# A new order table for a fused attention and two-layer kernel on one core

## The chip, the cores and the metric

The kernel runs on one core of a Trainium2 chip. The metric is the device time of one execution in microseconds. The engines spoken of are PE (TensorE, the 128 x 128 matmul array), DVE (VectorE), ACT (ScalarE), POOL (GpSimd) and SP (SyncE, which here only issues DMA transfers).

## The reference

For each of 4 batches of 12,480 tokens with 128 channels, 32 learned vectors attend to the tokens, and the tokens then attend to the 32 results. What comes out goes through two linear layers (128 to 2048 to 128) with a leaky rectifier that has one slope per hidden unit between them.

```
h   = mab(I, x)          # softmax(scale * I x^T) x, 32 rows
o   = mab(x, h)          # softmax(scale * x h^T) h, 12480 rows
u   = o @ w_in           # 128 -> 2048
g   = max(u, 0) + alpha * min(u, 0)
out = g @ w_out          # 2048 -> 128
```

## The kernel before

**Tiling.** Tokens are taken in groups of 512; a batch has 24 such groups and one of 192, so there are 100 groups in all. The 32 rows of h are multiplied into w_in once per batch (`hW`, 32 x 2048), so the first layer has a contraction of only 32: its operands are `hW` and the exponentials `rep`. Every matmul of both layers uses one *row tile* of the array, 32 of its 128 rows, and the four row tiles work side by side. The letters w, x, y and z name row tiles 0 to 3.

**Fill.** One `fill` computes 128 hidden units for 512 tokens: one matmul of `rep` and `hW` on one row tile into one of eight accumulation banks. ACT (line 772) or DVE (line 774) then applies the rectifier and writes the result to a buffer `gt` in bfloat16, which frees the bank. The table says which of the two does it. A full group has 16 fills.

**Second layer.** Each `gt` buffer has 128 rows, and `second` multiplies it with `W1` in four matmuls, one per row tile, all of which add into one bank that belongs to the group. A row tile's *part of a group* is 16 such matmuls. The parts of w, x, y and z follow each other on the group's bank: x begins when w has ended, and so on. Since two row tiles may not write one bank at once, `second` calls `hand_over` ahead of the first matmul of x, y and z: PE's queue waits there until the last matmul of the tile before has finished. Within a tile the parts of successive groups follow without a break. When z has ended its part, DVE transposes the bank (`ot`, line 845), POOL scales it (`ob`) and issues the stores. The last three groups take whole 128-row matmuls instead.

**The other work.** At 36 pauses, numbered by batch and 2048-token block, PE, ACT and DVE do the attention work of this and the next batch: scores and their exponentials (`bs`, `as`), sums into h (`aa`), denominators (`den`). Ahead of a batch's first group stands a chain: `hd` inverts the sums of the softmax (`rh`, `fr` on DVE), `ht` makes h (`hT`), `hw` multiplies h into w_in. SP then writes the exponentials to memory (`e2d`), reads them back to all four row tiles (`rep`) and does the same for the denominators (`rt`, `rdT`).

**Order.** All instructions are pinned to the order in which the code records them, on every engine. That order is the string `PLAN`: a to h with a digit is a fill (row tile by pairs of letters, the first of a pair evacuated by ACT, the second by DVE; the digit is the bank), w to z is the next second-layer matmul of that row tile, l opens a group's bank, v is a whole matmul, s is the next pause, and the digits after it are its banks. `PAUSES` lists what is done at each pause in order; `EVENTS` lists loads and transfers by group and fill.

```
        first = i < LATE and n == 0 and not r
        if r and n == 0:
            hand_over(left[i])
        ins = mm(
            home[i][:, :t], W1[rows, c, :], gt[rows, :],
            start=first, stop=False, skip_group_check=True,
        )
```

Of the kernel before, what the change touches and what calls it, by code (L numbers as in the profile page):

```python
# [38 lines left out]
20 8 bs06 aa15 den05 hd1  # L39
21 4 ht1  # L40
21 12 hw1 bs10 as20 den06 hl1
# [171 lines left out]
zyd3l6zyxwzya0xzyb1xzywxzya2zxyzxwys3012xh4ywxg3ywxywh0xywg2xe1wxwzf4xwzxwe3zxwzf2xwzc0wzd1wyzwy
c4zyza3yzxb2yzxl0yzxwyzc1b4yzxwyzxa3yzxwyg2xwyxwh1yxg4wyxwyxg3wyd7wxwe2zxwf1zxwzxwe4zxwf3zc7wzc2
ywzyd1zyxzya4xzb3yxza7yxzyxb2zyxzl1yxg4wyxwh3yxwg7yxzwyxzwyc2ywxg4yxwf3xwze7xwzxwf2s5437wyzd2wyz
c5wyzwyzd4we3zwyzb7yza2yzxya5zxyb4zxyl3zxywxzf7a2xzywxzywxg5ywxg4ywxyh2wxg7wxwxzf5wxze6wxze4wxzw
zd2wzywzc7ywzd6ywzyc5za4yzb2xyzxyl7zxywzxyb6g5xywzxywzxya4xywg2xywh6xywxywg5xwf4xwze0xwzf2xwze6x
wzwzd5ywzc4ywzc0ywzyl6zd2wzyxwzyxzya4xzyb5xzya0xzywxg2ywxzywxywh4xywg5xywxyg0wxs2154wxe0zwxf2zwx
e1zxwze4d5zwzywd0zywc2zyl1yzxwyzxa5zyxb4zyxwyzc2b0yzxwyzxa5yxwzyxwg4yxwg2yxwh0yxwyxwg5xwf4xzwe3x
zwxzwf2c0zwzd5ywyzwyzc4l3yzwxzya2xzyb0xzywxe5zwd4yzwxzya2xzywxzya0xywxh5ywxg4ywxywxg2ywxh0wxe7zw  # L220
xf4zwxzwe5c2zwyzwd0yzl7ywzxya4xzf5wzxywyzc2b0yzxwyzxa4yzxb5yzxwzyc2wzyxs0452ywxg0f6wxg4ywxg5ywxh
2ywxs0d6we4zxwzxwze5xwzf2c0wzd4zyl6yxzwxyza5xyzb2xyzwc0yzwxyzb4xyza5xyzwxyza2xyzwxywg0xyh4wxyg5x
wys21045wxywxh2e1wxf4zwc5zwyzwyc0zwyd1zwyc2zyzb5xyza4xyzl0xyzwxyza1xf2zwxzywxf4g5wxyzwxyza1xzywx
yg2wxyg5wxyh4wxwxf1zwxe3zwzwc2yzwyd5wzyc4wzyzl3d1yzwxyza2xyzwxf5zwxe4zwxyzb1xyza2xywzxyzwc5ywxyg
4wxyg1b2xywxywxe5b7xzwe4xzwd2zwxe1zwd5zwyc7zwyzc4yb2zxyl1zxywzxya5h7yxwzyxwg4d2ywzywxza5yxzyb7xz
xywg4ywxzywxg2yxwe5wxf7wzxf4xzws2657wxzf2wzc4wzyd6wzyc7l5zywwzxywwwzxe2b4zxywwzxywa7h6xywwxzywwx
zwe2wb4xyzwxwzya7xzyl6xywxg2ywxyh4wxywg7xywxwf0c2zwyxzxwxyxh4wc7yzxwyxzxwxe2d0zwyxzxwyxzwc7f4zxw
yxzxwyc2zb0yxzxxyza7xyzb4xyzxya2zxyzl0xywg7xywxyh4ywyxe2zwxyzwyxyyh3we7xzwyxyzywyxe4h2wxyzwyxyyz
wyc7f3zwyzwyc4zwyd2zwyzwc7yzyb3zxya4zxyzxa2yzxl7yzxzwyzzxa3zf4zxzwzyzxzwzyg2xywh1xwyzxg3wyxzzwxz
ze4wzxf2wzxwe1zxwzf3c5wzywzyc4wzyd2wzyc1zwyb3zyza5xyzxyb4zxya2zxyl1xzywxze3xwyh5xwyg4xwyxwyg2xwy  # L230
h3s6452xzwf3xzwe6xzwe4xzwf2xzwc5zwzwyd3wzywd6zywc4zya2zyl5zyxwh3yxwzyxwg4yxb6zyxwzyxa2yzxwyxwyg3
xwyxh4ya6xwe2xwxzf0wxzwxe3zwxzf6wzc4wzywd2zywc0zyzya3zxb6yzxyl4zxywzc2b0yzxywzxya3zxywg6xywxyh2w
xywg0xyg3wxywh7xwe6xzwxzwf2xzwe0xzwd3zwyzc7wyzwyza6d2yzl0xyzwxyg3wd7yzwxyzwxe6zb2xyzwxyza3xyzwxy
a7xywh6xyg2wxywxyg3wxf1wxwzxe7wzxf2zwc6zwyzwd3yzc1yzxa7yzxb2yzxl6yzxwyzc3b1yzxwyzxwyg7xb2yzxwyzx
we3zwxyg1wxywxywxh7ys23517xwzf2xwze3xwzf7c5wzwzyc1wzyd2wzya3zyzyxb7zyxa5zyxb1zyxl2zyxwze3xwzyd7w
yxg5wyxzwyxg1wyxg3wyxh7wyxwxg5wxzf1wxze4wxzwzd3wzyc7wzyd5wzyc1l4zyxwzyxa3zf7xwzyxwze1xzb5yxzwyxz
a3yxzwyxg7wyxwh1yxa5yxwg3yxwyxh0wyxwe7xwzf5wc1zywzywd3zywc0zya7zyxb5zyxl1zyxwzyc3b0zyxwzyxwg7f5x
wzyxwzyxa3zf0xwzyxwg7yxwzyxwg5yxwf3xwe0zxwzxwze7wd6zywzywc5yzd0l3zwxe7zwxzyb6xzywc5yzwxyzxb0yzxa
7zyxwyh6xa5yzxwyzxwyg0xwyxwg7yxwyh5xws60275h6we0xwzxwzd2e5zyc7wzywzyd0l6zyxwzyxa5zyd2wzyxwg7yxwz
f0xwzyxa5zyxwh2yxwze7xwzyxwh0yxa5yzxwyxza2yxg7wxwzxf0wze5wzywd2zywc4zya7zyxzb0yxzl5yxzwyxg2b4yxz  # L240
wyxzwyc7h0wyxzwyxza2yxh4wyxzwyc7zwyxzwe0xwf2zxwzxe4wzxwzxe7wzd0wzywzc1yl4zd2ywzxya7zxywh0xywzc1y
wzyxb2zyxa7zyxwzyxa0zyxwg1yxwyxwh2yxwg7yxwxf0we3xzwf1xzwze2xwzwzc7wyzd0yl3zwyxzya2xh1ywxzxya7zxy
b0zxywzc2wyzd1wyzxa7yzwxyzwxyg0wxyh2xwyg1wxye7wxwxzf0s6127f0zxwe6zxwzd1we7zwyzc2yzxyb0zxyzxya6zy
xb7zyxa1zyxl2zyd0wzyxwg6yxwh7yxwzyc1wzyxwg0yxwh6xywxwe7xzwxe1zwxzwf0c5zwyzwd7yzwc6yzwd1yza0yzxl5
yzxwyzxa7f6zxwyzxwyg0xb1yzxwyzxa7yzxwyg6xwyh0xwyxg1wyxwe7xwzxf4wzxe6wzwzyd1wzyc0wzyd7wzya4zya6xz
yxzb1yxzl0yxzwyd7zwe4xzwyxzwe6xzwyxg1wyxwh4yxwyg7xwyxh6wyxa3xe1wzxwzf4xwze7wzywzd3ywzc6yl1zyxwh4
yxwg7yxwzyxb3zyc6wzyxwzyxa4h7yxwzyxwzyd3a6zyxwzyxwg4yxwzxe7wzxwzxb6s34273e6wzd4f7wzxe2wzxs3yc6wz
yl4zd2ywzxya7zxzb3yxg6wyxywzxwyh2xyg7wxzwyxzb3yc6ywzxyzwxza2yxyg7wxwyxf6xg3wxwze2xwzf5zwzwyc7zwy
# [902 lines left out]
```

## Time and profile before

| what | value |
|---|---|
| time, 3 runs | 540.28, 542.75 and 543.44 us; median 542.75 us |
| the profiled execution | 540.08 us, with a span of 538.2 us from its first to its last instruction |
| PE busy | 523.0 us |
| DVE busy | 503.5 us |
| ACT busy | 495.8 us |
| POOL busy | 395.7 us |
| granted clock | 0.998 |

Busy time is the union of an engine's instructions, so that matmuls which run side by side count once, and an ACT or DVE instruction that starts before the one ahead has ended counts only for what it adds. A PE that is busy all the time can still have free row tiles.

### The profile page before, as it was taken

What the parts mean: (1) busy time and instruction counts of PE and PEld (TensorE: products, weight loads), DVE (VectorE), ACT (ScalarE), POOL (GpSimd) and SP (SyncE); (2) the same over time, 40 slices, a digit from 0 to 9 for tenths busy, and PEclk for the clock granted to TensorE, in tenths of its full rate; (3) what the DMA queues carried; (4) which work ended last, traced back from release to release, by engine and by line L of the source; (5) the groups of instructions that cost most, each with busy time, mean ns of one, the idle gap of its engine ahead of it and who ended that gap; (6) DMA issues with size and microseconds to landing.
All of it is one profiled execution on the core that took longest, in us unless ns stands there. A gap on an engine that the chain in (4) does not pass through costs nothing.

```text
span 538.2 us, 21998 instructions
## 1 busy us (share of the span) xinstructions
PE 523.0 (97%) x9275; PEld 333.5 (62%) x9276; DVE 503.5 (94%) x865; ACT 495.8 (92%) x994; POOL 395.7 (74%) x574
## 2 busy tenths in 40 slices
PE   4999999999999999999999999999999999999995
PEld 4655566666567666666667666666666566666652
DVE  3699999999999999999999999999999999999994
ACT  2499999999999999999999999999999999999950
POOL 5553777787678988688687987776777877776764
PEclk9999999999999999999999999999999999999999
DMA  8998999986898988787799797855344344334324
GB/s 196 213 185 138 163 198 149 185 141 117 131 170 144 146 152 151 163 129 143 116 161 161 123 163 154 157 114 113 67 93 113 66 95 113 70 90 108 66 43 85
DMA packets 114738, 71.14 MB, mean 132 GB/s; under 512 B 86784, under 2 KB 102784, under 8 KB 114640
## 3 DMA queue, kind: packets, MB, share of 16 engines
q0 software_dynamic: 19456, 38.62, 39.0%
q1 hardware_dynamic: 91984, 30.22, 32.9%
q8 instruction: 72, 1.18, 1.0%
q10 hardware_dynamic: 3200, 0.90, 0.7%
q14 instruction: 26, 0.21, 0.1%
HBM read 41.00 MB, written 28.95 MB: 130 GB/s over the span
## 4 chain that ended last, share of the span: by engine, by line
PE 90%; DMA 4%; DVE 2%; ACT 2%; POOL 1%; issue 1%; SPq 0%; POOLq 0%; DVEq 0%
PE bank L385 90%; DMA xn<-in_x_dram 2%; ACT gt L772 1%; DVE gt L774 1%; DMA rep<-e2d 1%; POOL xn L414 1%; DVE ot L845 0%; DVE xT L463 0%; SPq L673 0%; PE bank L460 0%; DVE fr L610 0%; DVE ob L853 0%; POOL out_dram L878 0%; ACT e L658 0%; ACT rep L683 0%
## 5 line engine op out<-in xcount | busy, mean ns | idle before, releaser
L385 PE MATMUL bank<-gt,W 32*128 32x512 bf16 x6255 | 478.7, 371 | 0.3 <-ACT e L658 0.2
L772 ACT ACTIVATE gt<-bank 128x512 bf16<-128x512 f32 (+1 forms) x906 | 464.1, 617 | 5.6 <-PE bank L385 3.7
L774 DVE TENSOR_SCALAR gt<-bank 128x512 bf16<-128x512 f32 (+1 forms) x662 | 417.5, 678 | 8.7 <-PE bank L385 5.0
L385 PE MATMUL bank<-rep,hW 32*128 32x512 bf16 (+1 forms) x1600 | 418.9, 368 | 0.5 <-DMA rep<-e2d 0.3
L385 PEld LDWEIGHTS <-W 32*128 32x128 bf16 x6256 | 264.6, 92 | 145.1 <-issue 43.5
L878 POOL DMA_DIRECT2D out_dram<-ob x386 | 248.1, 672 | 37.0 <-POOL ob L853 29.4
L853 POOL TENSOR_TENSOR ob<-ot,rdT 128x512 f32<-128x512 f32 (+2 forms) x99 | 106.6, 1077 | 90.8 <-DVE ot L845 88.1
L385 PEld LDWEIGHTS <-hW 32*128 32x128 bf16 x1600 | 136.8, 92 | 19.9 <-issue 5.5
L845 DVE STREAM_TRANSPOSE ot<-bank 128x512 f32<-128x512 f32 (+1 forms) x100 | 69.9, 699 | 5.0 <-PE bank L385 4.0
L385 PE MATMUL bank<-rep,hA 32*128 32x512 bf16 (+1 forms) x100 | 36.1, 367 | 0.0
L429 POOL DMA_DIRECT2D xn<-in_x_dram x32 | 20.7, 663 | 0.1
L483 ACT ACTIVATE e1t<-bank 128x256 bf16<-128x256 f32 (+2 forms) x14 | 5.0, 358 | 10.9 <-PE bank L385 10.9
L463 DVE COPY xT<-bank 128x1024 bf16<-128x1024 bf16 (+1 forms) x13 | 8.4, 651 | 5.1 <-PE bank L460 4.6
L385 PE MATMUL bank<-xT 32*128 32x512 bf16 x81 | 12.5, 376 | 0.0
L555 ACT ACTIVATE e<-bank 128x512 bf16<-128x512 f32 x18 | 11.1, 616 | 0.2 <-PE bank L385 0.2
L658 ACT ACTIVATE e<-bank 128x512 bf16<-128x512 f32 x18 | 11.1, 617 | 0.1
L385 PEld LDWEIGHTS <-xT 128*128 128x128 bf16 (+1 forms) x177 | 7.9, 95 | 4.3 <-issue 1.5
L385 PEld LDWEIGHTS <-hT 128*32 128x32 bf16 (+1 forms) x122 | 3.7, 93 | 10.9 <-issue 10.8
L385 PE MATMUL bank<-xT,hT 128*32 128x512 bf16 (+1 forms) x98 | 10.3, 388 | 0.0
L385 PEld LDWEIGHTS <-hA 32*128 32x128 bf16 x100 | 9.2, 92 | 1.7 <-issue 0.8
L460 PE MATMUL bank<-ident,xn 128*128 128x128 bf16 x96 | 8.6, 242 | 1.4 <-DVE xn L990 0.9
L414 POOL DMA_DIRECT2D xn<-in_x_dram x11 | 6.2, 581 | 3.3 <-DMA xn<-in_x_dram 2.5
(87 smaller groups left out, 133.9 us busy)
## 6 DMA issues: line engine op xcount, KB each, us to landing
out_dram<-ob POOLq DMA_DIRECT2D x373, 64.0 KB, 3.3
rep<-e2d SPq DMA_DIRECT2D x92, 128.0 KB, 3.8
xn<-in_x_dram POOLq DMA_DIRECT2D x37, 256.0 KB, 5.3
e2d<-e SPq DMA_DIRECT2D x24, 128.0 KB, 3.3
xn<-in_x_dram POOLq DMA_DIRECT2D x4, 512.0 KB, 6.1
rdT<-rt SPq DMA_DIRECT2D x96, 8.0 KB, 2.7
early<-in_moe_w_out_dram POOLq DMA_DIRECT2D x4, 256.0 KB
xT<-xn SPq DMA_TRANSPOSE x36, 5.1
```

Source lines behind the costliest of these rows:

```text
L385: return pin(nc.tensor.matmul(o, lhsT, rhs, start=start, stop=stop, **kw))
L414: pin(nc.gpsimd.dma_start(out=xn[:, q0:q1, :], in_=src[:, q0:q1, :]))
L429: pin(nc.gpsimd.dma_start(out=st.xn[u][:, part, :], in_=src[:, part, :]))
L460: pin(nc.tensor.transpose(tp[:, k * P : (k + 1) * P], xn[:, q, j * C : (j + 1) * C], ident[:]))
L463: pin(nc.vector.tensor_copy(out=st.xT[:, u, qs[0] : qs[-1] + 1, :].rearrange("c q t -> c (q t)"), in_=tp[:, : len(qs) * GRP],))
L555: pin(nc.scalar.activation(out=e1[:], in_=ps[:], func=EXP, scale=scale, accum_out=st.es[:, u : u + 1]))
L658: pin(nc.scalar.activation(out=e2[:].rearrange("p (t j i) -> p t j i", j=n, i=32), in_=turned(ps[:pp, :w], n), func=EXP, scale=scale_of(st ...
L772: pin(nc.scalar.activation(out=gt[:, :w], in_=ps[:, :w], func=RELU))
L774: pin(nc.vector.tensor_relu(gt[:, :w], ps[:, :w]))
L845: pin(nc.vector.transpose(out=ot[:, :t], in_=acc[:, :t]))
L853: pin(engine.tensor_tensor(out=ob[:, k0 * w : k1 * w].rearrange("p (k m c) -> p k m c", k=k1 - k0, c=32), in0=ot[:, k0 * w : k1 * w].rearr ...
L878: pin(queue.dma_start(out=dst[a], in_=ob[32 * a : 32 * a + 32, :t].rearrange("p (b k) -> p b k", k=32),))
```

## The change

The first 54 fills stay as they are; the rest of the string `PLAN` is new. It holds the same operations: 1568 fills, 6208 matmuls of the second layer on row tiles and 48 whole ones, 100 opened banks and 36 pauses. 900 fills go to ACT and 668 to DVE, where 906 and 662 did. In `PAUSES`, three numbers change; the pauses themselves are where the string has its s.

```
-20 8 bs06 aa15 den05 hd1
-21 4 ht1
-21 12 hw1 bs10 as20 den06 hl1
+20 4 bs06 aa15 den05 hd1
+21 0 ht1
+21 8 hw1 bs10 as20 den06 hl1
...
-wxe3wh5x2w32wc43wyd13wyc6wg3ys5b4yya1d6ywya5yyg3xb43xy3ya1xyxh6yc53yxh3ya4x3xy3xb1xza6zl5xe7zwxf
+2w32wc43wyd13wyc6wg3ys5b4yya1d6ywya5yyg3xb43xy3ya1xyxh6yc53yxh3ya4x3xy3l7xf1wxwe6zxzb5zxc3wwzzxwh4c1
...
```

The changed file is four lines shorter ahead of its code, so that line 774 of before is line 770 of the change, and so on.

**First place: a hand-over on PE.** This is the start of y's part of a group just behind the pause with `bs12`; `bank_97` is the group's bank before, and `bank_96` after. PE_49 is PE's own semaphore, by which a hand-over waits; Activation_49 and DVE_49 are those of ACT and DVE. The weight loads that stand ahead of each matmul are left out, but for the one that has the hand-over's wait. Before:

```order
L385 MATMUL bank_97<-gt_146,W_253 128x512
L385 MATMUL bank_90<-gt_169,W_253 128x512
L385 MATMUL bank_91<-gt_137,W_253 128x512
L385 MATMUL bank_95<-rep,hW 128x512 [waits Activation_49]
L385 MATMUL bank_90<-gt_102,W_253 128x512
L385 MATMUL bank_91<-gt_145,W_253 128x512
L385 MATMUL bank_90<-gt_122,W_253 128x512
L385 MATMUL bank_91<-gt_135,W_253 128x512
L385 LDWEIGHTS W_253 [waits PE_49]
L385 MATMUL bank_97<-gt_143,W_253 128x512
```

After:

```order
L381 MATMUL bank_96<-gt_120,W_253 128x512
L381 MATMUL bank_96<-gt_152,W_253 128x512
L381 MATMUL bank_97<-gt_115,W_253 128x512
L381 MATMUL bank_93<-gt_155,W_253 128x512
...
L381 MATMUL bank_93<-gt_104,W_253 128x512
L381 MATMUL bank_93<-gt_123,W_253 128x512
L381 MATMUL bank_94<-rep,hW 128x512 [waits Activation_49]
L381 LDWEIGHTS W_253 [waits PE_49]
L381 MATMUL bank_96<-gt_134,W_253 128x512
```

Before, the first row is the last matmul of x's part, and y's first stands eight places behind it. After, x's last two matmuls stand directly behind each other, and y's first comes eleven places behind the second of them.

**Second place: repeats of a row tile on PE.** These are rows behind the pause with `bs24`; again without weight loads. Before, where bank_96 is y's, bank_95 is x's and bank_92 is w's:

```order
L385 MATMUL bank_90<-rep,hW 128x512 [waits DVE_49]
L385 MATMUL bank_96<-gt_170,W_253 128x512
L385 MATMUL bank_95<-gt_172,W_253 128x512
L385 MATMUL bank_92<-gt_132,W_253 128x512
L385 MATMUL bank_95<-gt_163,W_253 128x512
L385 MATMUL bank_91<-rep,hW 128x512 [waits DVE_49]
L385 MATMUL bank_96<-gt_158,W_253 128x512
```

After, where bank_91 is y's and bank_95 is x's, and the two fills are both of z:

```order
L381 MATMUL bank_95<-gt_108,W_253 128x512
L381 MATMUL bank_91<-gt_159,W_253 128x512
L381 MATMUL bank_94<-rep,hW 128x512 [waits DVE_49]
L381 MATMUL bank_92<-rep,hW 128x512 [waits Activation_49]
L381 MATMUL bank_91<-gt_105,W_253 128x512
L381 MATMUL bank_95<-gt_128,W_253 128x512
L381 MATMUL bank_95<-gt_141,W_253 128x512
L381 MATMUL bank_91<-gt_165,W_253 128x512
```

Before, hardly two neighbours in the string have one row tile; after, two fills of z and two matmuls of x stand directly behind each other. Over the whole order 125 matmuls follow directly on one of the same row tile before, and 1100 after; two places behind it 293 and 1216, three places 1466 and 1334, four places 4757 and 1379.

**Third place: the chain ahead of batch 1 on DVE.** `rh` and `fr` belong to `hd1`, `hT` to `ht1`. Before:

```order
L586 TENSOR_TENSOR hacc<-bank_94,hacc 128x128
L701 RECIPROCAL rd<-bank_95 128x16
L608 RECIPROCAL rh<-bank_92 128x1
L610 TENSOR_SCALAR fr<-fold,rh 128x128
L774 TENSOR_SCALAR gt_124<-bank_96 128x512
L774 TENSOR_SCALAR gt_126<-bank_92 128x512
L617 CAST hT_3272<-bank_90 128x128
```

After:

```order
L604 RECIPROCAL rh<-bank_92 128x1
L606 TENSOR_SCALAR fr<-fold,rh 128x128
L770 TENSOR_SCALAR gt_176<-bank_95 128x512
L770 TENSOR_SCALAR gt_115<-bank_94 128x512
L770 TENSOR_SCALAR gt_171<-bank_95 128x512
L770 TENSOR_SCALAR gt_129<-bank_94 128x512
L770 TENSOR_SCALAR gt_173<-bank_90 128x512
L770 TENSOR_SCALAR gt_177<-bank_91 128x512
L841 STREAM_TRANSPOSE ot<-bank_97 128x512
L613 CAST hT_3264<-bank_94 128x128
```

Two evacuations stood between `fr` and `hT` before, and six and a transpose do now. In the string, the pause with `hd1` comes after 324 fills where it came after 336, the one with `ht1` after 339 for 341, and the one with `hw1` after 344 for 356. So 15 fills lie between the first two, where there were 5, and 5 between the last two, where there were 15. SP's transfers keep their order, and so do POOL's, but for one load of `xn` (block 2 of batch 2) that now stands ahead of one group's `ob` and stores instead of behind them.

More of the change, by code (lines that the diff above doesn't have):

```diff
@@ L302 @@
[L302 to L303 removed]
+b02h12c223a312s4h212b012a323c12313f413s23e01h112l2wg42d33w231w3e03w32d1w31we431w3f31w3e01w32w3d12w3c
+42w32wd3g02w132w12h1wc4232xa02h3xa523x23b4x23a1x23xl0w23wxxwf3g5xw3e4s1h5xe3wxe4w3xwf13xw23xwxe3wh5x
+2w32wc43wyd13wyc6wg3ys5b4yya1d6ywya5yyg3xb43xy3ya1xyxh6yc53yxh3ya4x3xy3l7xf1wxwe6zxzb5zxc3wwzzxwh4c1
+xwzwzwf6e5wwxg3xzxzb1c4zwwyzb5c6yzywwwyc3f1yzzc4wzl5yzxxwg6xywyh3a1yyxwyxwwf4c2yxa6wyxxb3yxg1yyxh4xw
@@ new lines @@
+we2xxwf6zs314zwf2xzxwwzxe6f3wzzc4wywh1yc2wyyzzyd6c3yyzzxb4zxyg1yxzya2xb6yxxza3yxzzl1yxzyxg4ywxwywh2w
+e6xxxwg3zwf0wzwzxze4xxf2we6wzwzyd3c0yzzyyzwwwd4wyc2zzywzya6zb3yxxzya0yzzyl4xwxg2yxyxwh6wa3yyywxwxxh0
+g7wxwze2wzxxf6zc3wxwzxf7ze0xzwwxh2ws637d0zzwyywc2wyd6zza3yyzyxb7zxa0zzxyyyzxa2xl6zxyywxg3xywwh7g0wxx
+yywxwh2yxwg5ywwxxe3f7xwzxe0wzzwf2zzc5wywyzd3yc7zwwyzzyd0l2yxza5xzzwxyyb3xzya7ywxzxyh0a5wxyxzyxwyzg3y
+wxywxg7wxh0e5xwxzzwf3wxe1xzwzf7wzwc0zzyywywzc5d3wzzya1yzyxb7yxyxza0b5xzzyl3xyc1zyxwzxyg7yyxwwh0wxg5y
@@ new lines @@
+ywxxwwh1e4wxzs705zxb4e1wzxxe7zwf5zxc0zwzwwyd1zzwc4ywywzd7ya5yzzzyxa0xyb1xzyl4yzxwg7wyzxywg5wyxxxyg0w
+h1xyyxwyh7xwe6xwwxb5zzxe1e0xxwwwzzd6wzze7ywwyzd1zwc5zzyyyd0a6xxzya7zyxzyzb1yxxl5wzyxg0wzwxyg6xxywwyy
+h7a1yxyxh0wxwe2xwwxzxe6zwzf7xwze1wzyzd2wyzc0wzwwyyd6zzl7yc1wzyxxzya2zb0yzxyxzwa6xzyxwys1206wyh3xwg1y
+xg2wxyywh6wxyxxe0wf3wze1zwxxwxzf2xwc6wzzwyd0wc3yzyzza1xb2zzyyyxxl6zwd0a3xyxwyzyzb2zc1xwwyzzyxg3yywyg
+0xxwwxh1wxg2yyxxwwf3ze4wxwzf0xzxzwe1wzd2wwyzc3zyc4yzxyzb0yzxa1zyxxb3a2yzxzxyl4xyh0ywxwze1wyxzxzc3wyw
@@ L304 @@
+wzc7zyd0zl1wyyzxzxa5yh4xyxwwzyc7xzb0xzyywg5wxywzd4wyg7wyxwzxxyg0yb5xyzzwxa4zwxyys70e5wzwxzf4xwze7xf2
+wzwzc0yd5zyxzya4yzyxxxzza7b2zzl0wyyyxxc4h5xywwzyxywg7d2wzxyza4zxywyxyg5wxywg7xs2f4wxwzxze6xf5wzze2zz
+wwwyd7yc4wyzwc6yyzyyzd5a2zzxxyxb7zyxa4zyxxzza6zyxyxg2xyxyyh5yg4xxg7h6xze3xze2xzxzf5f4zzyd6yza7zyzzyz
+yb3d5zzyb2yyyzzyzh4h7yym6h3yyvvvvvvvvvvvvvvvvyb5d2d1ym4h7h3vvvvvvvvvvvvvvvvzb6zd5zd2b1zzzm7f3zzzzf4z
+zzzzzvvvvvvvvvvvvvvvv
 """
```

182 lines of the change are left out of this document (80 added, 102 removed).

## The prediction

> **What bounds the kernel now.** I read the windows first, then the groups of instructions, then the waits of the engines that empty banks.
>
> ```profile
> core 0: us, PE busy (x) PEld busy (x) DVE busy (x) ACT busy (x) POOL busy (x), PEclk, DMA share, GB/s
> 100.00:200.00 100.00, 99.51 (x1853) 64.58 (x1854) 96.98 (x170) 97.89 (x201) 79.45 (x113) 1.00 0.88 149
> 200.00:300.00 100.00, 99.99 (x1845) 66.44 (x1839) 96.42 (x165) 99.13 (x197) 77.14 (x110) 1.00 0.83 144
> 400.00:500.00 100.00, 99.97 (x1800) 63.43 (x1798) 98.52 (x164) 99.54 (x197) 75.53 (x105) 1.00 0.40 91
> ```
>
> Three engines are full at once: ACT to 98 or 99%, DVE to 96 to 98%, PE by its union. POOL and the DMA queues have room.
>
> ```profile
> L772 ACT ACTIVATE gt<-bank 128x512 bf16<-128x512 f32 (+1 forms) x906 | 464.1, 617 | 5.6 <-PE bank L385 3.7
> L774 DVE TENSOR_SCALAR gt<-bank 128x512 bf16<-128x512 f32 (+1 forms) x662 | 417.5, 678 | 8.7 <-PE bank L385 5.0
> ```
>
> An evacuation takes ACT 464.1/906 = 0.512 us and DVE 417.5/662 = 0.631 us of its own time (the means of one overlap). Together they empty a bank every 0.283 us. Most of the span is 1568 such banks, so a new order can gain only where one of the two stands idle or slow. The waits between 45 and 505 us say how much idleness that is:
>
> ```profile
> ACT gt L772 <- PE bank L385: 2.7, 8, 0.6
> DVE gt L774 <- PE bank L385: 3.6, 11, 0.6
> DVE ot L845 <- PE bank L385: 1.8, 8, 0.5
> ```
>
> 8.1 us on two engines that share the work: 4.05 us of span, if all of it went. There is some slowness beside it, which looks busy:
>
> ```profile
> 299.57 4.12 ACT L772 ACTIVATE gt<-bank 128x512 bf16<-128x512 f32 x8
> 487.01 18.95 ACT L772 ACTIVATE gt<-bank 128x512 bf16<-128x512 f32 x37
> ```
>
> Without the overlap of about 0.11 at its end, the long stretch has 0.509 us for each and the short one 0.501. If all 900 went at 0.501 instead of 0.512, ACT would have 10 us less; that is the far end of any gain.
>
> **Hand-overs.** PE's timeline at the first place of the order, before:
>
> ```profile
> 177.46 0.38 PE L385 MATMUL bank<-gt,W 32*128 32x512 bf16 x3
> 177.53 0.37 PE L385 MATMUL bank<-rep,hW 32*128 32x512 bf16 x1
> 177.67 0.38 PE L385 MATMUL bank<-gt,W 32*128 32x512 bf16 x3
> 177.74 0.37 PE L385 MATMUL bank<-rep,hW 32*128 32x512 bf16 x1
> 177.89 0.38 PE L385 MATMUL bank<-gt,W 32*128 32x512 bf16 x3
> 178.11 0.37 PE L385 MATMUL bank<-rep,hW 32*128 32x512 bf16 x1
> 178.11 0.60 PE L385 MATMUL bank<-gt,W 32*128 32x512 bf16 x4
> 178.33 0.39 PE L385 MATMUL bank<-rep,hW 32*128 32x512 bf16 x1
> ```
>
> Each row tile starts a matmul every 0.216 us, so four tiles take a place of the order in 0.054. x ends its part with the matmul at 177.89. The fill of 177.74 is y's last before the hand-over; y's next start is among those of 178.33, 0.44 after x's last. A hand-over thus wants 0.434 us or eight places. Counted in the strings, 177 of 291 hand-overs stand closer than eight places before and 87 after. The sum of what is lacking (0.434 less 0.054 for each place) is 16.3 us of PE before and 8.2 after: half goes. Of the 8.1 us of idleness, 2.25 us belong to batch 1's chain (next part); the other 5.85 are 2.9 us of span. I give hand-overs the half of all of it: **-1.5 us** (bounds 0, if the other tiles' matmuls cover the waits, and -2.9).
>
> **Batch 1's chain.**
>
> ```profile
> 132.91 0.83 DVE L610 TENSOR_SCALAR fr<-fold,rh 128x128 f32<-128x128 f32 x1
> 132.97 1.58 ACT L772 ACTIVATE gt<-bank 128x512 bf16<-128x512 f32 x3 [0.55 <-PE bank L385]
> 134.88 1.58 ACT L772 ACTIVATE gt<-bank 128x512 bf16<-128x512 f32 x3 [0.33 <-PE bank L385]
> 136.63 3.19 ACT L772 ACTIVATE gt<-bank 128x512 bf16<-128x512 f32 x6 [0.18 <-PE bank L385]
> 140.74 1.29 DVE L774 TENSOR_SCALAR gt<-bank 128x512 bf16<-128x512 f32 x2 [0.28 <-PE bank L385]
> ...
> 136.29 2.64 SPq L673 DMA_DIRECT2D rep<-e2d  x4
> 139.04 2.20 SPq L715 DMA_DIRECT2D rdT<-rt  x4
> 141.34 0.39 SPq L665 DMA_DIRECT2D e2d<-e  x1
> 143.80 1.95 SPq L673 DMA_DIRECT2D rep<-e2d  x4
> ...
> 151.01 0.38 PE L385 MATMUL bank<-rep,hW 32*128 32x512 bf16 x1 [0.30 <-DMA rep<-e2d]
> 151.43 4.69 ACT L772 ACTIVATE gt<-bank 128x512 bf16<-128x512 f32 x9 [0.49 <-PE bank L385]
> 151.51 2.76 DVE L774 TENSOR_SCALAR gt<-bank 128x512 bf16<-128x512 f32 x4 [0.42 <-PE bank L385]
> ```
>
> Before, PE comes to `ht1` five fills after `hd1`, while DVE still makes `fr`, and ACT loses 1.06 us. After, 15 fills (4.2 us) lie between: that wait goes. What is late next is `hw1`: it stands 5 fills (1.4 us) behind `ht1` and needs `hT` from DVE, which is queued behind a transpose; with that late, PE holds back every fill behind it. I charge 0.3 us (bounds 0 and 1.1, the loss that moves here). The second loss is at 151.0, where batch 1's first `rep` lands 0.3 us late. SP issues it behind the transfers of the last block of batch 0, which hang on that block's exponentials; these come 12 fills, or 3.4 us, earlier, SP's order is the same, so `rep` lands ahead of its use. That returns 0.49 us on ACT and 0.42 on DVE, and DVE's 0.28 at 140.7. Sum: 1.06 and 0.49 on ACT and 0.70 on DVE, 2.25 on two engines, 1.1 of span; less 0.3: **-0.8 us**. The load that POOL issues earlier is off this path.
>
> **Six fills from ACT to DVE.** ACT gains 6 x 0.512 = 3.1, DVE pays 6 x 0.631 = 3.8. DVE is idle more, so it could be a gain of up to 3.1; if DVE sets the pace it costs 3.8. I take half the difference, **+0.35 us**. The last ACT fill is the 1550th instead of the 1552nd; the whole matmuls behind it are the same.
>
> **Repeats of a row tile.** In each stretch of 32 row-tile matmuls an even order gives 8 to each tile. The fullest tile has 9.11 on average before and 9.38 after, 63 steps more over the whole order: 63 x 0.216 = 13.6 us of PE. What hides them is that row tiles stand free: of the 1800 matmuls between 400 and 500 us about 100 belong to pauses, and 1700 x 0.054 = 92 us, so 6 to 8 in 100 are free. The rest is that a fill comes late when its own tile has just been given a matmul: 206 fills stood three places or less behind one, and 526 do now. At 0.054 a place that is 38 us more of lateness over 1500 fills. It is felt only where the emptying engine has nothing queued: 27 idle waits (the rows above) among some 1480 evacuations, 1.8%, so 0.7 us on two engines: **+0.35 us** (bounds 0 and 13.6).
>
> That a repeat does not hold up the other tiles can be seen at the second place:
>
> ```profile
> 344.16 0.37 PE L385 MATMUL bank<-gt,W 32*128 32x512 bf16 x1
> 344.30 0.37 PE L385 MATMUL bank<-rep,hW 32*128 32x512 bf16 x1
> 344.31 0.44 PE L385 MATMUL bank<-gt,W 32*128 32x512 bf16 x3
> 344.52 0.37 PE L385 MATMUL bank<-rep,hW 32*128 32x512 bf16 x1
> ```
>
> Four second-layer matmuls stand between the two fills in the order, the second x among them, and only three have started when the second fill starts at 344.52: the fill has overtaken the x whose tile was busy. The Trainium skill (TensorE: Matmul & The Clock Gate, "Part 3: Packing small matmuls — row/col tiling") says that matmuls start strictly in program order. By that rule each repeat would hold back all behind it; these rows do not agree with it.
>
> **The sum.** -1.5 - 0.8 + 0.35 + 0.35 = -1.6 us. The profiled execution took 540.08 us with its 538.2 us span, so it would be 538.5; it is 2.7 below the median of the three runs, 542.75, against which the sum gives **541.2 us**.
>
> **Rivals.** *The row tiles decide.* A fill that waits behind its own tile lengthens its bank's round (fill, evacuation, next fill). About 4.3 fills lie between two uses of a bank in the string; if the rounds set the pace, the 38 us of lateness are 38/4.3 = 8.8 us of span: 550. It decides from the point where ACT's idle time before `gt` passes about 10 us (5.6 now). For it: ACT does wait for PE. Against it: only eight times in 460 us. *The slowness goes too.* If hand-overs also cause what makes ACT take 0.512 where 0.501 is possible, half of those 10 us come on top: 541.2 - 5.2 = 536.0. For it: 291 hand-overs are spread over the whole span; against it: the best stretch of 8 is short. *The change doesn't do what it says.* Hand-overs were covered by matmuls that the other tiles still had, and only the chain's 0.8 and the two charges are left: 542.7. *Strict program order*, held back by the 975 more neighbours and the 923 more at two places, would cost 975 x 0.162 + 923 x 0.108 = 258 us: 800; the row of 344.52 speaks against it.
>
> **How the numbers follow.** Forecast 0.31, no effect of hand-overs 0.13, slowness goes too 0.27, row tiles decide 0.28, strict order 0.01. Faster by over 1%, about what a measurement of this kernel can tell from no change, is below 537.3: 0.27. Within 1%: 0.31 + 0.13 = 0.44. Slower: 0.29. The range reaches from 532 (the far end of the slowness, 541.2 less 10) to 552 (the row tiles, 550, with some of the 13.6 us). The forecast alone would be 538 to 545.
>
> **What would show it.** Right: ACT's 0.55 us wait near 133 us and the one at 151 us are gone; the waits of ACT and DVE for PE between 45 and 505 us fall from 8.1 to about 4 us; ACT's own time for an evacuation stays near 0.51. Wrong: more idle time before `gt` on both engines, a longer one than 0.512 on ACT, or a new wait at `hw1`.

## The result and the profile after

The changed kernel takes 538.60 us (median of 21 runs, 537.27 to 542.93); the kernel before, run beside it, takes 540.66 us (21 runs, 539.51 to 543.44). The ratio is 0.9963, with a 95% interval from 0.9947 to 0.9979: 2.0 us less, between 1.1 and 2.9. The prediction was 1.6 us less. Below, a change in microseconds is always the ratio less one, times the median of before in the same comparison.

The groups of the changed kernel's page (line 768 is ACT's evacuation, 770 DVE's, 841 the transpose of a group's bank; busy us, mean ns of one, idle us ahead of them):

```profile
L768 ACT ACTIVATE gt<-bank 128x512 bf16<-128x512 f32 (+1 forms) x900 | 460.8, 606 | 7.2 <-PE bank L381 4.7
L770 DVE TENSOR_SCALAR gt<-bank 128x512 bf16<-128x512 f32 (+1 forms) x668 | 416.1, 677 | 9.4 <-PE bank L381 6.2
L841 DVE STREAM_TRANSPOSE ot<-bank 128x512 f32<-128x512 f32 (+1 forms) x100 | 70.0, 700 | 3.3 <-PE bank L381 2.2
```

ACT's evacuation still takes 460.8/900 = 0.512 us. DVE's takes 416.1/668 = 0.623 us where it took 0.631: DVE does six more in 1.4 us less. ACT does six fewer in 3.3 us less. The idle time has not shrunk: 16.6 us ahead of the two evacuations, where it was 14.3, and 1.7 us less ahead of the transposes (5.0 before). The waits between 45 and 505 us say the same (in total, times, longest):

```profile
ACT gt L768 <- PE bank L381: 3.4, 10, 0.8
DVE gt L770 <- PE bank L381: 4.8, 14, 0.9
DVE ot L841 <- PE bank L381: 0.5, 3, 0.2
```

8.7 us where it was 8.1. Of the 8.7, 1.7 us (0.80 on ACT, 0.88 on DVE) belong to one stop of PE near 177 us that before's profile doesn't have, and for which the trace names no cause:

```profile
177.27 0.37 PE L381 MATMUL bank<-gt,W 32*128 32x512 bf16 x1 [0.56 <-issue]
```

Without it, 7.0 us would be left, far from half. So the gain is not in the waits that I had counted. What did shrink is the spacing of DVE's evacuations, which the page counts as busy time. Of DVE's evacuations of 512 columns that directly follow another one, 334 of 526 start less than 0.62 us behind it before, and 403 of 531 after. Part of the wide ones are short waits for PE that the lists don't show: between the 120th and the 1490th evacuation, 147 of 452 such evacuations start within 0.06 us of the end of their own fill before, and 93 of 458 after, as far as the modelled ends of matmuls can tell, and those that do are spaced by 0.65 to 0.66 us.

Where along the span it comes from is seen in the windows from 410 to 505 us; the first two rows are before's, the last two the change's:

```profile
410.00:470.00 60.00, 60.00 (x1073) 37.45 (x1072) 59.42 (x99) 59.88 (x118) 45.41 (x64) 1.00 0.39 91
470.00:505.00 35.00, 35.00 (x618) 22.12 (x609) 34.81 (x58) 34.99 (x70) 26.78 (x37) 1.00 0.43 96
```

```profile
410.00:470.00 60.00, 60.00 (x1083) 40.20 (x1080) 59.59 (x100) 59.90 (x120) 45.55 (x65) 1.00 0.40 92
470.00:505.00 35.00, 35.00 (x630) 23.81 (x622) 34.85 (x59) 34.98 (x70) 26.52 (x37) 1.00 0.43 97
```

All engines are as full as before, and yet ten and twelve more matmuls fit in: 60 x 10/1073 + 35 x 12/618 = 1.2 us. From 170 to 410 us nothing is won in these two profiles: summed over four stretches of 60 us, the change's trace has 4423 matmuls there and before's 4438. The stop near 177 us is in that part; across it, the change's lead over before goes from 0.73 us to nothing.

The other way to see it is to count evacuations of ACT and DVE in order of their start in the trace, and to compare when the k-th starts. Change less before, in us: 340th -0.05, 440th -0.73, 640th +0.05, 1240th +0.02, 1490th -0.66, 1567th -1.35; the span is 1.2 shorter. The first of these differences come and go; the last two stages, fills 1240 to 1490 and the last 78, keep theirs. Profiles of one order differ by less there: over these stages the runs below that have before's order in them (the new head in both, the new end and the six fills alone in the first) stay within 0.1 us of before.

The end itself changed. Before, from DVE's timeline:

```profile
523.29 0.72 DVE L845 STREAM_TRANSPOSE ot<-bank 128x512 f32<-128x512 f32 x1 [0.71 <-PE bank L385]
527.38 0.72 DVE L845 STREAM_TRANSPOSE ot<-bank 128x512 f32<-128x512 f32 x1 [1.41 <-PE bank L385]
528.94 0.56 DVE L774 TENSOR_SCALAR gt<-bank 128x384 bf16<-128x384 f32 x1 [0.40 <-PE bank L385]
529.80 1.49 DVE L774 TENSOR_SCALAR gt<-bank 128x384 bf16<-128x384 f32 x3 [0.31 <-PE bank L385]
```

After:

```profile
522.36 0.72 DVE L841 STREAM_TRANSPOSE ot<-bank 128x512 f32<-128x512 f32 x1 [0.75 <-PE bank L381]
526.45 0.72 DVE L841 STREAM_TRANSPOSE ot<-bank 128x512 f32<-128x512 f32 x1 [0.68 <-PE bank L381]
527.10 2.84 DVE L770 TENSOR_SCALAR gt<-bank 128x384 bf16<-128x384 f32 x6
```

DVE's waits behind the whole matmuls shrink from 0.71 + 1.41 + 0.40 + 0.31 to 0.75 + 0.68, and the last six evacuations run without a pause.

Batch 1's chain did as it was meant to. ACT after, around it:

```profile
129.42 6.22 ACT L768 ACTIVATE gt<-bank 128x512 bf16<-128x512 f32 x12 [0.41 <-PE bank L381]
135.51 0.62 ACT L654 ACTIVATE e<-bank 128x512 bf16<-128x512 f32 x1
136.00 0.62 ACT L551 ACTIVATE e<-bank 128x512 bf16<-128x512 f32 x1
136.47 0.22 ACT L551 ACTIVATION_READ_ACCUMULATOR e<-bank 128x1 f32 x1
136.66 15.43 ACT L768 ACTIVATE gt<-bank 128x512 bf16<-128x512 f32 x31
```

The 0.55, 0.33 and 0.18 us of before are gone, and so is the 0.49 at 151 us; a wait of 0.41 is there in their place, ahead of the chain.

### The profile page after: what moved, and what is told of

It is laid out like the page before. It is cut to its first block, busy times and chain, and to the rows that moved or that the text cites. A ratio compares the mean times of both kernels' runs of the same rounds, so it can differ in the third digit from the quotient of the medians.

```text
span 537.0 us, 22004 instructions
## 1 busy us (share of the span) xinstructions
PE 522.1 (97%) x9276; PEld 346.0 (64%) x9276; DVE 502.8 (94%) x871; ACT 492.9 (92%) x988; POOL 394.9 (74%) x574
## 4 chain that ended last, share of the span: by engine, by line
PE 54%; POOL 26%; issue 10%; DMA 4%; DVE 3%; SPq 2%; ACT 1%; POOLq 0%; ACTq 0%; DVEq 0%
PE bank L381 52%; POOL out_dram L874 17%; POOL ob L849 8%; PE bank L456 1%; DVE gt L770 1%; DMA e2d<-e 1%; DMA ind_f<-in_inducing_dram 1%; SPq L711 1%; DMA rdT<-rt 1%; SPq L669 1%; DMA rt<-rd 1%; DMA rep<-e2d 1%; DVE xT L459 0%; DMA out_dram<-ob 0%; DVE ot L841 0%
## 5 line engine op out<-in xcount | busy, mean ns | idle before, releaser
L381 PE MATMUL bank<-gt,W 32*128 32x512 bf16 (+1 forms) x6256 | 478.2, 371 | 0.7 <-issue 0.6
L768 ACT ACTIVATE gt<-bank 128x512 bf16<-128x512 f32 (+1 forms) x900 | 460.8, 606 | 7.2 <-PE bank L381 4.7
L770 DVE TENSOR_SCALAR gt<-bank 128x512 bf16<-128x512 f32 (+1 forms) x668 | 416.1, 677 | 9.4 <-PE bank L381 6.2
L381 PEld LDWEIGHTS <-W 32*128 32x128 bf16 x6256 | 273.2, 92 | 130.5 <-issue 34.5
```

The source lines that it names most:

```text
L381: return pin(nc.tensor.matmul(o, lhsT, rhs, start=start, stop=stop, **kw))
L768: pin(nc.scalar.activation(out=gt[:, :w], in_=ps[:, :w], func=RELU))
L770: pin(nc.vector.tensor_relu(gt[:, :w], ps[:, :w]))
```

## The experiments

Four theories stood. **H**: hand-overs that stand further apart give the gain (my largest term). **C**: batch 1's chain gives it. **S**: six fills fewer on ACT give it. **F**: the order is one fit of fills, engines, banks and second-layer matmuls; the gain lies in the stretches where the new fit is better, and no single property carries it. Beside them stood the rival of the prediction that the row tiles decide. In the diffs the strings are pieces of `PLAN`; the first of several places is shown.

**Six fills alone.** Fills 126, 243, 273, 804, 1549 and 1552 of the kernel before go from ACT to DVE, which gives the change's 900 and 668:

```diff
-0yzxa3yzxwzxywxg7ywxg4ywyxh0wyg3
+0yzxa3yzxwzxywxh7ywxg4ywyxh0wyg3
...
```

> The kernel before with nothing changed but six letters: six fills go to DVE instead of ACT (four in the body, the two at 1549 and 1552 at the end), as many as the new order moves; row tiles, hand-overs, pauses and banks stay. Theory S (the gain of the new order is that ACT has six fills less to empty, about 3 us of its work, of which idle time takes some back): 1 to 2 us faster than before, ratio 0.996 to 0.998. Theory H (the gain comes from hand-overs that stand farther apart): no faster than before, ratio 1.000 to 1.002, the recorded sum has +0.35 us for it. Theory C (batch 1's chain and the first quarter): the same as H here.

Measured: 1.0065 (1.0049 to 1.0081), 3.5 us slower. The 1567th evacuation starts 3.1 us later than before, 0.96 of it behind the 1490th, where the last two letters stand. ACT waits longer for PE:

```profile
ACT gt L772 <- PE bank L385: 5.1, 14, 0.6
DVE gt L774 <- PE bank L385: 3.6, 12, 0.6
```

**Six fills back.** The other way round, in the change: fills 118, 247, 270, 800, 1547 and 1552 go back to ACT.

```diff
-ze0xzwwxh2ws637d
+ze0xzwwxg2ws637d
...
```

> The changed kernel with six fills given back to ACT at about the same places (906 and 662 again); hand-overs, repeats and the chain are those of the new order. Theory S: the gain is gone, 0.999 to 1.002 of the kernel before. Theory H: still 1.5 to 2.5 us faster than before, ratio 0.995 to 0.997. Theory C: the same as H.

Measured: 1.0000 (0.9984 to 1.0017); the whole gain is gone. That is what S expected here, and it speaks against H and C, since hand-overs and chain are the change's. But S had the run above wrong. Moving six letters costs 3.5 us in the one order and 2.0 in the other (1.0000 less the change's 0.9963), though in opposite directions: 0.3 to 0.6 us for each. So S by itself falls, and so does any price of the assignment by itself: it belongs to its order. Without the six letters the rest of the new order wins nothing either (-0.9 to +0.9 us). The page of this run says why the two may need each other:

```profile
L772 ACT ACTIVATE gt<-bank 128x512 bf16<-128x512 f32 (+1 forms) x906 | 463.5, 607 | 6.1 <-PE bank L385 3.8
L774 DVE TENSOR_SCALAR gt<-bank 128x512 bf16<-128x512 f32 (+1 forms) x662 | 412.5, 676 | 11.5 <-PE bank L385 8.3
```

DVE's evacuations are as close as in the change (412.5/662 = 0.623 us), which leaves DVE 5.0 us more room than before, but ACT has its 906 again and is as full as before (463.5 us; 464.1). In the run above, where the order is the old one, DVE's evacuations stay at 420.5/668 = 0.629 us, and its six more come on top. So the new order makes room on DVE, and the six letters put it to use; that this is the whole of it is not shown. The five kernels with the new order from fill 432 on (the change, this run and three below) all have 0.622 to 0.624 us, and the nine others 0.628 to 0.635.

**The new head alone.** The change up to fill 439, with its chain, and before's order from there:

```diff
-...xzzywyxwg6f1wyxyyzzwxe5wxyh0xxzzwywyye6y
+...xzzywyxwg6e1xzwyxyzywyxe5h0wxyzwyxyyzwyc
```

> The new order up to fill 439 (some 167 us), with the moved chain ahead of batch 1 and two of the six fills, then the order of before. Theory C: the chain's idle time at 133 and 151 us is what the change saves, so 0.8 to 1.1 us faster, ratio 0.998, and the gain stays to the end. Theory S: two of six fills, 0.5 us or less, 0.999 to 1.000. Theory H: a quarter of its 1.5 us, 0.999.

Measured: 1.0002 (0.9985 to 1.0019). The span of the profile is 537.5 us, 0.7 less than before's, with the 1240th evacuation 0.5 us earlier; the times show no gain, with -0.8 us just inside the interval.

**The new end alone.** Before up to fill 1494, and the change's end:

```diff
-...xg7ywywxh4ywxg1ywxwf2xzxe3wzxf7wzxwe4zwc
+...xg7ywywxh4wyxg1ywf2xwe3xwzxwzwf7xe4xwzwz
```

> The order of before up to fill 1494 (some 500 us), then the end of the new order: the last 74 fills, with one fill less for ACT and the last two groups' fills put otherwise between the whole matmuls. Theory S: one fill of six, 0.3 us. Theory T (the end is where it is gained: in the profiles the last fill is emptied 1.35 us earlier, while at fill 1340 the two are 0.2 us apart): 1 us or more faster, ratio 0.998 or less. Theories H and C: no difference.

Measured: 0.9991 (0.9979 to 1.0004). In its trace the 1490th evacuation is 0.95 us later than before's and the 1567th 0.27 later: 0.7 us come back in the last 78, as in the change itself (-0.66 to -1.35). The times have -0.5 us (-1.1 to +0.2): they agree with 0.7, but not with theory T of this run, by which the end gives 1 us or more, unless at the edge of the interval.

**Hand-overs apart.** Before, with matmuls that follow a close hand-over moved back in the string:

```diff
-zyc3zyxb7zyxg2yxb4zyxza1yxzyxb3ze7xzyxl2yxwg4y
+zyc3zyb7zyxxg2yxb4zyxza1yxzyxb3ze7xzyxl2yxwg4y
...
```

> The kernel before, with the second-layer matmuls between neighbouring fills exchanged so that each hand-over stands further behind the end of the part before it: 10.2 places on average instead of 7.7, and 14 of 291 closer than eight places instead of 177. Fills, their engines, their banks and the pauses stay. Theory H (the change gains by its hand-overs, as my prediction's largest term says): the shortfall falls from 16.3 to 2.2 us of PE, more than in the change, so at least the -1.5 us of the prediction: a ratio to before of 0.995 to 0.9975. Theory F (the gain comes from the fit of fills, engines and banks in the last third): 0.999 to 1.001. A price of repeats shows as more than 1.001, since 208 matmuls follow directly on one of their row tile instead of 110.

Measured: 1.0171 (1.0151 to 1.0192), 9.2 us slower. No theory had this. The edit did more than my expectation says: 269 matmuls also passed one or two fills. The waits for PE between 45 and 505 us grew from 8.1 to 13.5 us:

```profile
DVE gt L774 <- PE bank L385: 6.1, 23, 0.6
DVE ot L845 <- PE bank L385: 2.1, 9, 0.5
...
ACT gt L772 <- PE bank L385: 5.3, 20, 0.6
```

**The new last third.** Before up to fill 1225, the change from there:

```diff
-...0xzxwze7zwc5zwyd3wzywc2yzyzd7wya0zyzxb5y
+...0xzxwze7zwd5yc3wzyywzc2zwd0wzzya7yyxzb3a
```

> The kernel before up to fill 1225, and the change's order from there, with banks and buffers renamed at the seam. The milestones of the two profiles put 0.45 us of the gain between fills 1340 and 1490 and 0.7 us behind fill 1490. Theory F: these two are the whole gain, so -1.1 to -2 us, a ratio of 0.996 to 0.998. Theory C (the chain of batch 1 gives it, as the prediction's second term says, and the rest is scatter): 0.999 to 1.001. Theory H expects about a fifth of the hand-overs' gain, -0.3 us.

Measured: 0.9995 (0.9984 to 1.0006), so F's forecast of 0.996 to 0.998 is missed, and 0.999 to 1.001, which C had, is met. Its trace agrees with F all the same: the evacuation is 0.94 us later than before's at the 1240th, 0.62 at the 1490th and 0.07 earlier at the 1567th, so 1.0 us is won from fill 1240 on. Its times show less than that. The 0.9 us by which it was behind at the 1240th come from one stop near 149 us, in the part of the order that it shares with before (ACT's row, then PE's):

```profile
149.74 7.59 ACT L772 ACTIVATE gt<-bank 128x512 bf16<-128x512 f32 x16 [1.75 <-PE bank L385]
150.38 0.24 PE L385 MATMUL bank<-rep,hW 32*128 32x192 bf16 x1 [1.23 <-ACT gt L772]
```

PE holds at the 192-token fills of batch 0's last group. ACT, named as the releaser, had nothing to do since 148; a `rep` that landed late is likelier, but no row names it.

**Repeats of a row tile.** Before, with matmuls between two neighbouring fills exchanged so that letters repeat:

```diff
-e6zwh7xwzc3wzxwg4d1wzxwe6xzwf7zwzc3ywywzd4ywzc
+e6zwh7zwxc3xwzwg4d1xwzwe6xzwf7wzzc3yywwzd4zwyc
...
```

> The kernel before, with the second-layer matmuls between neighbouring fills reordered so that row tiles repeat: 1490 follow directly on one of their row tile (110 before by the same count, 1100 in the change) and 1005 two places behind one (354 before). Hand-overs keep their distance; fills, engines, banks and pauses stay. My prediction charged the repeats +0.35 us: a ratio of 1.000 to 1.002. The rival that row tiles decide: +8.8 us or more, 1.016 and up. Strict program order: over +250 us.

Measured: 1.0136 (1.0117 to 1.0154), 7.3 us slower. Repeats that are put in blindly do cost. It is not the price of the rival that the row tiles decide, though: by its rule the fills of this run are 21 us later than before's, counted in the strings, and 21/4.3 = 4.8 us would be lost; the change's fills are 38 us later, and it is faster.

**The change made even.** The change, with matmuls exchanged between neighbouring fills so that letters alternate:

```diff
-wf6e5wwxg3xzxzb1c4zwwyzb5c6yzywwwyc3f1yzzc4wzl
+wf6e5wxwg3xzxzb1c4wzwyzb5c6ywzywywc3f1zyzc4wzl
...
```

> The change, with the second-layer matmuls between neighbouring fills reordered so that row tiles alternate: 268 follow directly on one of their row tile instead of 1087; hand-overs keep their mean distance of 9.2 places, and fills, engines, banks and pauses stay. If repeats cost what the prediction says, this is 0.35 us faster than the change: 0.994 to 0.996 of before. If the new order lives by how its second-layer matmuls stand to its fills, it is slower than the change: 0.998 or more. If repeats don't matter, it is the same as the change, 0.9963 within 0.0016.

Measured: 537.42 us, 0.9953 (0.9938 to 0.9968). That is faster than before by 2.5 us; whether it is faster than the change (0.9963) the intervals don't tell. The 820 repeats fewer are worth 0.5 us at the most likely, with an uncertainty of about 1.2 us either way, where 1380 more cost 7.3 in the order before. A repeat has no price of its own: the new order has its 1087 where they cost little. (Counted over fills and row-tile matmuls of the second layer alone, as here, before has 110 direct repeats and the change 1087.)

**Hand-overs apart, in place.** As above, but no matmul passes a fill:

```diff
-7zwzc3ywywzd4ywzc1yzl6yxwg7yxg3wxywh4xywxya1xy
+7zwzc3wyzwyd4wyzc1yzl6wyxg7yxg3wyxwh4yxwyxa1yx
...
```

> The kernel before with hand-overs moved apart again, but now only second-layer matmuls between two neighbouring fills change places with each other: no fill, engine, bank or pause moves, and no matmul passes a fill. 42 of 291 hand-overs stand closer than eight places (177 before), the shortfall falls from 16.5 to 4.9 us of PE, further than in the change. Direct repeats of a row tile fall too (45 for 110), those at two places rise (478 for 354). Theory H (hand-overs give the gain; the +9 us of the first try came from its matmuls passing fills): -1.5 us or more, 0.995 to 0.9975. Theory F (the gain is the fit of fills, engines and banks, and hand-overs are covered): 0.999 to 1.001. Theory S (any exchange off the found order costs, as it did with the six fills): above 1.002.

Measured: 1.0029 (1.0013 to 1.0044), 1.6 us slower. Fewer close hand-overs than the change has (42 to 87), fewer direct repeats than before, the fills where they were, and no gain. What a hand-over costs PE can be read from the trace: it is the wait of PE's weight loads for PE's own matmuls. Between 45 and 505 us, for before, the change and this run:

```profile
PEld L385 <- PE bank L385: 11.8, 55, 0.3
...
PEld L381 <- PE bank L381: 7.5, 34, 0.3
...
PEld L385 <- PE bank L385: 4.4, 21, 0.3
```

So the waits at hand-overs did fall, in the change and further here, but the waits of the emptying engines for PE rose, from 8.1 to 9.8 us here:

```profile
DVE gt L774 <- PE bank L385: 4.1, 11, 0.6
DVE ot L845 <- PE bank L385: 2.1, 9, 0.4
...
ACT gt L772 <- PE bank L385: 3.6, 10, 0.7
```

H as I had it falls: time that PE's queue no longer stands at hand-overs did not come back as less waiting on ACT and DVE. That the other row tiles' matmuls cover it is the likely reason, which no run shows by itself. The theory called S in this expectation is another one than above: any exchange off a found order costs. It expected more than 1.002, and fits.

**The new order without its head.** Before up to fill 432, with its own chain, then the change:

```diff
-...0yxzxxyza7xyzb4xyzxya2zxyzl0xywg7xywxyh4
+...0yxzxxyza7yzxb4yxxza2yxzyl0zywxg7ywxyh4y
```

> The kernel before up to fill 432, with its own chain of batch 1, and the change's order from there. The part of the gain that comes before fill 432, the chain above all, is taken out. Theory F: the middle carries what the last third alone did not, so nearly the whole gain: 0.9955 to 0.9975. My prediction's terms: without the chain's -0.8 us, a ratio of 0.998 to 0.999. If the gain needs the whole order, 0.999 to 1.001.

Measured: 0.9966 (0.9950 to 0.9981), 1.8 us faster: about all of the gain without the new chain, as F expected. With the head alone at 1.0002, C falls as the cause of the gain; that the head gives a part of it is not excluded, since the intervals reach 0.8 us. In its trace the evacuations are 0.32 us earlier than before's at the 1240th, 1.00 at the 1490th and 1.70 at the 1567th, so the last third gives 1.4 us here, against 1.0 in the run of the last third alone.

**The change with both evened.** Letters alternate and hand-overs stand apart, without passing a fill:

```diff
-wf6e5wwxg3xzxzb1c4zwwyzb5c6yzywwwyc3f1yzzc4wzl
+wf6e5wxwg3xzxzb1c4zwwzyb5c6ywzywywc3f1zyzc4wzl
...
```

> The change, with second-layer matmuls exchanged only between neighbouring fills, so that both row tiles alternate (172 direct repeats for 1087) and hand-overs stand apart (36 of 291 closer than eight places for 87; shortfall 3.9 us for 8.3). If hand-overs and repeats both cost, as the prediction's terms say: 0.9925 to 0.9945 of before, better than the change. If neither matters here, 0.995 to 0.997. If exchanges off the found order cost: 0.998 or more.

Measured: median 538.74 us, 0.9996 (0.9969 to 1.0022): inconclusive, since its times fall into two groups, eight from 537.38 to 538.91 and four from 542.34 to 544.03. The first group is no better than the change.

**What had cost 9.2 us.** The counterpart of the first hand-over try: the same shifts, but of the seventh matmul of a part instead of the first:

```diff
-xb3ze7xzyxl2yxwg4yxwyxwg1yxwh3yxwxg7wf4xzwxe0z
+xb3ze7zyl2yxxwg4yxwyxwg1yxwh3yxwxg7wf4xzwxe0zw
...
```

> The counterpart of e3_handovers, without its hand-overs: in the kernel before, the seventh matmul of a tile's part of a group is moved back where e3 moved the first, so 237 of the 6208 second-layer matmuls stand one or two fills later (269 in e3), with 209 direct repeats and 645 at two places (208 and 678 in e3); hand-overs stay close, 183 of 291 under eight places. If e3's +9.2 us comes from matmuls that stand later against the fills (and from the repeats that this makes), this one loses as much: 1.011 to 1.019; what it loses beyond e3 is then what the wide hand-overs give back. If e3's loss comes from row tiles that pause at a hand-over, this one stays at 1.000 to 1.005.

Measured: 1.0206 (1.0192 to 1.0220), 11.1 us slower, with the waits for PE grown as in the first try and more:

```profile
DVE gt L774 <- PE bank L385: 10.3, 38, 1.0
DVE ot L845 <- PE bank L385: 3.0, 13, 0.5
...
ACT gt L772 <- PE bank L385: 6.4, 19, 1.0
```

So the loss was not one of hand-overs: it comes with matmuls that stand later against the fills. A simple estimate, made after the runs, is near its size. A matmul moved back by n places leaves its row tile without work for n x 0.054 us, and one of four tiles idle is a quarter of PE. Counted in the strings, the first try moved the first matmuls of the parts back by 657 places in all, 657 x 0.054/4 = 8.9 us (9.2 measured); this one the seventh ones by 737, 9.9 us (11.1 measured).

It is no rule, however. Counted over every second-layer matmul that stands later, the run in place has 1321 places and the one with repeats 3414, which would be 17.8 and 46 us; 1.6 and 7.3 were measured. What only the two dear runs share is that matmuls pass fills, 269 of them in the first try and 237 here. Why that makes the engines wait so long is not shown. The two tries differ by 1.9 us, which could be what the wide hand-overs give back, but the run in place has the other sign; so the value of hand-overs in the order before stays open, within about 2 us either way.

## Why the prediction was right, and where it was not

The difference came out right (541.2 against 542.75, -1.6; measured -2.0), but most of the terms did not. They were wrong in ways that cancelled, and that the sum is within 0.4 us is luck. By two of its own signs the mechanism was wrong: the waits did not fall to about 4 us, and there is more idle time ahead of `gt` on both engines (7.2 and 9.4 us; 5.6 and 8.7 before). The time itself, 541.2 us, is 2.6 too high, mostly because the median of three runs that it starts from is 2.1 above that of the 21.

- **The bound.** That ACT and DVE are full, and that a new order can gain little where nothing but 8 us of waits is to be had, was right: no version gained more than 2.5 us. I looked for the rest of the slowness on ACT (0.512 against 0.501 us). It was on DVE: 0.631 to 0.623 us, 662 x 0.0077 = 5.1 us of DVE's time, which pays for its six more evacuations (3.7 us) and leaves 1.4, while ACT, with six fewer, has 3.3 us less to do.
- **Hand-overs, -1.5 us.** The failed step is "I give hand-overs the half of all of it". It made a bound into a value: that PE stands less at hand-overs says nothing of the emptying engines if other row tiles cover it. PE's waits there did fall, from 11.8 to 7.5 us in the traces (16.3 to 8.2 in my count), but those of ACT and DVE did not (8.1 to 8.7 us), and with 4.4 us at hand-overs the run in place was 1.6 us slower. The change's own hand-overs with the six fills back gave nothing.
- **Batch 1's chain, -0.8 us.** The waits that I named are gone, at 133 and at 151 us, and the feared one at `hw1` did not come. But the head with it alone gives 0.1 us more time (-0.8 to +1.0), and the order without it has the whole gain. What is won at 151 us differs from run to run: ACT lost 0.49 us there in before's profile, 0.89 in that of the order without the new head, and 0.72 to 1.75 just ahead of it in three others with the old head; of the five with the new head none lost more than 0.32.
- **Six fills, +0.35 us.** Priced as if the rest of the order stood still. With the rest standing still it costs 3.5 us, near the 3.8 us of my bound; in the new order six at about the same places are worth 2.0 us to keep, all of the gain. The term cannot be told apart from the order.
- **Repeats, +0.35 us.** In the new order the size was right: made even, it is 0.5 us faster, if at all. (Its bound of 13.6 us depends on where the stretches of 32 begin; counted again in the strings, there are 26 to 44 steps more, not 63. The bound is no part of the sum.) As a rule it was wrong, since the same kind of repeats in before's order costs 7.3 us. The weight that I used, 27 idle waits among 1480 evacuations, was taken from before's order and then held for any place. What makes the new order's repeats cheap is not shown; 145 of its fills stand directly behind a matmul of their own row tile, where 24 did before, so it does not keep them away from fills.
- **The end, at nothing.** That "the whole matmuls behind it are the same" was true and beside the point: the evacuations between them are ordered differently, and the last 78 fills give 0.7 us in the traces, a third of the gain, in the change, in the new end alone and in the order without its head. With the six fills back, two of which are there, they give 0.1.
- **The rivals.** *The slowness goes too* (536.0) was wrong on ACT; the change has no more than the 5.1 us on DVE named above. *The change doesn't do what it says*, with hand-overs at no effect, is nearer the mechanism than my forecast, but it kept the chain's gain and missed the end's. *The row tiles decide* did not come, but row tiles do weigh: repeats put in blindly lost 7.3 us, and matmuls moved past fills 9.2 and 11.1, neither at that rival's price. *Strict program order* priced repeats at 258 us for the change; 1380 more direct repeats and 651 more at two places cost 7.3 us here, where by that rule they would cost 1380 x 0.162 + 651 x 0.108 = 294. The traces say it directly: in the change's, 476 of the 1600 matmuls of fills start ahead of one to six second-layer matmuls that stand before them in the order. The rule of the Trainium skill (TensorE: Matmul & The Clock Gate, "Part 3: Packing small matmuls — row/col tiling") that matmuls start in program order does not hold for different row tiles in this kernel.

What stays open: the gain is 1.0 to 1.4 us from fill 1240 on in the five traces that have the new fills there unaltered, but the times of the last third alone show 0.3 us (-0.9 to +0.3). The 0.6 to 1.0 us that are left of the change's 2.0 have no sure place: in four of the five traces with the new head (the fifth has the six fills back), the evacuations near fill 440 are 0.6 to 1.0 us ahead of before's, but the times of the new head alone show nothing (-0.8 to +1.0). Which property makes DVE's evacuations closer isn't settled either. It is not the repeats or the hand-overs, since the two evened orders keep 0.622 to 0.623 us with other repeats, and one of them with other hand-overs. Short waits for PE are only a part, since the count of evacuations that start right behind their fill is as low (85 to 98) in the three orders that lost 7 to 11 us. F says that it is no property alone; the square of the six letters and the two orders agrees with that, and the other runs agree without proving it.

## What to carry to other kernels

When the engines that set the pace are 97% full and a change replaces a whole searched order, price it as one thing by the idle time that is left (here 4 us of span), not as a sum of properties: the same kind of move, six fills from ACT to DVE, cost 3.5 us in one order and was needed for the whole gain in the other. Look at the spacing of an engine's instructions in what the page calls busy, not only at its listed waits: the room that the new order made on DVE was there. Be careful with matmuls that move past fills: two runs that did so with some 250 of 6208 lost 9 and 11 us. And look at the end of the program on its own: in the traces, the last 5% of the fills gave a third of the gain.

## What the runs showed of the hardware

- Matmuls on other row tiles overtake a repeat (476 of the 1600 matmuls of fills start out of order in the change's trace), but not for nothing: 1380 more direct repeats cost 7.3 us, 5 ns for each, where a full wait would be 162 ns.
- A late transposing load can cost more than its wait. In the profile of the change made even, PE stands still 1.79 us for `xT`, last issued at 190.10, and in the stretches from 196 and 200 us the granted clock falls to 0.81 and 0.76 (the column behind the five engines):

```profile
197.92 0.39 PE L385 MATMUL bank<-xT,IT 128*32 128x512 bf16 x2 [1.79 <-DMA xT<-xn]
```

```profile
192.00:196.00 4.00, 4.00 (x84) 2.24 (x77) 3.97 (x7) 3.96 (x9) 3.70 (x6) 1.00 1.45 96
196.00:200.00 4.00, 2.21 (x40) 1.19 (x41) 1.43 (x4) 1.92 (x6) 3.15 (x5) 0.81 0.91 209
200.00:204.00 4.00, 4.00 (x59) 2.83 (x55) 3.03 (x5) 2.93 (x6) 0.00 (x0) 0.76 0.75 92
```

That execution took 540.49 us where the median of its kernel is 537.42, so the pause and the slow stretch behind it cost about 3 us; in its trace, the evacuations lose 3.4 us on before's between the 520th and the 560th. In stretches of 2 us the clock is 0.62 from 198 and 0.53 from 200, and 1.00 again from 202. It is one execution: in the profile of the run with six fills back, PE stands still 1.41 us for `xT` ahead of 219.07, and the clock stays at 1.00.
